# Another order for 2,801 steps: the copy of the sums of phi and v moves up in ScalarE's queue

## The chip, the cores and the metric

The kernel runs on one core of a Trainium2 chip. The metric is the device time of one execution in microseconds (us), lower is better, and the median of several runs is given. TensorE is named PE in the profile (PEld is its loading of weights), VectorE DVE, ScalarE ACT, GpSimd POOL and SyncE SP; SP issues nearly all the transfers between DRAM and the chip's memory.

## The reference

One layer in float32 over x of 2048 rows and 512 columns. Two halves, each with a layer norm, a scale and a shift from a small conditioning vector:

```python
mod = (silu(c) @ w_mod)                       # sa, ca, ga, sb, cb, gb: six rows of 512
h = layernorm(x) * (1 + ca) + sa
# A: linear attention, 32 heads of 16, with a learned feature map
pq, pk = q @ w_phi, k @ w_phi                 # per head
phi = concat([softmax(p), softmax(-p)])       # for q and for k: 32 features per head
kv, z = phi_k^T @ v, sum over rows of phi_k   # per head
A = (phi_q @ kv) / (phi_q . z + 1e-6)
x = x + ga * (A @ wo)
h = layernorm(x) * (1 + cb) + sb
# B: shift mixer and MLP
g = gelu(layernorm(h) @ w1)                   # four column groups shifted by +1, -1, +2, -2 rows
x1 = h + shifted(g) @ w2
B = x1 + gelu(layernorm(x1) @ w3) @ w4        # 512 -> 1376 -> 512
out = x + gb * B
```

## The kernel before

**Stages.** The rows are worked on in 8 chunks of 256 (two tiles of 128 rows). First stage, per chunk: norm, transposition, projection to k, v and q features (w_phi is folded into the weights ahead of it); per tile the products of the k features with v are summed on PE in one PSUM tile named `kva`, and the k features are summed in `za`. Only when all 16 tiles have been added can `kva` be read: ACT copies it to `kvs` (line "`act(kvs, kva)`" of the group "kvb"), PE spreads it out with four small products, and DVE multiplies the result with a mask into `const` (the matrix `kvb` of the code). Second stage, per chunk: the q features e, which went to DRAM, are loaded transposed by blocks, multiplied with the sums of the k features (`ez`) and reduced into the denominators (`pz`), normalised in place (`e`), turned by DVE (`pT`) and multiplied on PE with `kvb`; then wo, a norm, w1 with gelu, and the shift mixer with w2. Third stage, four times: the MLP for 512 rows, with seven products in place of eight for each pair of blocks (sums and differences of blocks first). Each float32 product in the large matmuls is made of three products of rounded high and low parts, so every operand has a "hi" (a copy) and a "lo" (source less hi).

**What sets the order.** The program is built in two passes. The first one records 2,801 steps (`plan.op`), each with its engine, its other possible engines and what it reads and writes; the step numbers are the same in both kernels. The second emits the steps in the order of a table `ORDER`, a list of step numbers written into the file. A letter behind a number (A, V, G) puts that step on ACT, DVE or POOL in place of its first engine. Each engine works through its own steps strictly in this order, so a step that waits holds up all that stand behind it on its engine. A second table, `SLOT`, says in which buffer every tile lies (one character for each tile of a name); a tile put into a used buffer waits until the last reader of the earlier tile is done.

```python
    def order(self):
        engines = {"A": "Activation", "V": "DVE", "G": "Pool"}
        for word in ORDER.split():
            o = self.ops[int(word.rstrip("AVG"))]
            if not word.isdigit():
                o.fn = o.alts[engines[word[-1]]][1]
            yield o
```

Names that the prediction uses: `qe` are the q features while they are made (`qt` is the copy of their projection; `q` and `k` with small shapes are minima, maxima and sums), `ke` the k features, `vv` the copy of v, `w` weights split in hi and lo, `ws` sums of blocks of w3 made for the third stage, `acc` the rows of the conditioning vector while they are summed up. Most of the helpers have one line each: L401 ACT's copies and exponentials, L418 DVE's and L420 POOL's two-operand operations, L442 DVE's reductions, L471 the matmuls.

Of the kernel before, what the change touches and what calls it, by code (L numbers as in the profile page):

```python
# [164 lines left out]
)  # L165
SLOT = {
    "pp": "015632614340517032150643012526242367251411661166312763426267553575313027152161025567307111272635"
          "0055072172642262056",
    "bd": "85",
    "w": "125634cd180254b6d83c72",  # L170
    "rk": "72634eg9",
# [1216 lines left out]
```

## Time and profile before

| | us |
|---|---|
| median of 3 runs | 558.26 (556.95 to 558.59) |
| the profiled execution's own time | 557.92 |
| its span, first to last instruction | 556.1 |
| PE busy | 545.4 (98% of the span) |
| DVE busy | 487.7 (88%) |
| ACT busy | 350.1 (63%) |
| POOL busy | 345.1 (62%) |

A row of the timeline gives the start in us from the span's beginning, the length of the group, engine, line, operation, output and inputs with their sizes, how many instructions were merged, and in square brackets the idle time of the engine before it with what ended that. A row of the windows gives, for a stretch, its length and the busy time of each engine in it. The granted clock of PE was 0.999 of full speed over the span.

### The profile page before, as it was taken

How to read it: one execution, taken by the hardware profiler on the slowest of the kernel's cores; microseconds unless marked ns; L12 is line 12 of the kernel's file. 1: busy time of each engine (PE TensorE's matmuls, PEld its weight loads, DVE VectorE, ACT ScalarE, POOL GpSimd, SP SyncE). 2: the span in 40 equal slices, each digit the busy share in tenths (PEclk: the TensorE clock that was granted, in tenths of full speed). 3: DMA queues.
4: the chain of work that ended last, by engine and by line, in shares of the span. 5: the costliest groups of instructions: out<-in, count | busy, mean ns of one | idle time of the engine just before them, and what ended most of it. 6: DMA issues, size and time to landing. Idle time of an engine off the chain costs nothing.

```text
span 556.1 us, 12353 instructions
## 1 busy us (share of the span) xinstructions
PE 545.4 (98%) x4498; PEld 488.6 (88%) x4498; DVE 487.7 (88%) x898; ACT 350.1 (63%) x831; POOL 345.1 (62%) x353
## 2 busy tenths in 40 slices
PE   8999999999989999999999999999999999999996
PEld 6988788888757788888889898999999999999996
DVE  3999999999999999999989867997878978786785
ACT  1899998635336778888888794966543365344530
POOL 2289976969489999999882655334332453333521
PEclk9999999999999999999999999999999999999999
DMA  8983366456447676779888798996678882972122
GB/s 317 366 279 133 127 197 226 154 153 181 156 126 255 207 204 196 248 242 312 267 262 272 245 306 297 383 326 211 276 238 308 286 330 66 294 246 81 57 78 76
DMA packets 63749, 124.90 MB, mean 225 GB/s; under 512 B 7140, under 2 KB 26852, under 8 KB 59592
## 3 DMA queue, kind: packets, MB, share of 16 engines
q1 hardware_dynamic: 63400, 124.04, 67.2%
q8 instruction: 35, 0.57, 0.4%
q14 instruction: 26, 0.21, 0.1%
q10 hardware_dynamic: 288, 0.07, 0.1%
HBM read 89.74 MB, written 34.35 MB: 223 GB/s over the span
## 4 chain that ended last, share of the span: by engine, by line
PE 86%; DVE 7%; DMA 3%; POOL 2%; issue 1%; DVEq 0%; ACT 0%; POOLq 0%
PE pp L471 36%; PE pa L471 27%; PE ac L471 20%; PE pt L480 2%; DVE pz L442 1%; DMA mod<-in_wmod 1%; DVE q L442 1%; PE kva L471 1%; POOL qe L420 1%; DVE pT L762 1%; DMA wr<-in_w 1%; POOL e L420 1%; DMA const<-in_id 1%; DVE ws L418 0%; DVE ez L418 0%
## 5 line engine op out<-in xcount | busy, mean ns | idle before, releaser
L471 PE MATMUL pp<-w,hh 128*128 128x512 f32 x576 | 138.3, 397 | 0.0
L471 PEld LDWEIGHTS pp<-w,hh 128*128 128x128 f32 x576 | 106.9, 188 | 25.6 <-issue 1.6
L471 PE MATMUL pa<-bH,wq 128*128 128x256 f32 x840 | 106.7, 282 | 0.0
L471 PE MATMUL ac<-w,gg 128*128 128x256 f32 x840 | 106.1, 281 | 0.0
L471 PEld LDWEIGHTS ac<-w,gg 128*128 128x128 f32 x840 | 103.2, 189 | 1.3
L471 PEld LDWEIGHTS pa<-bH,wq 128*128 128x128 f32 x840 | 103.1, 189 | 0.6
L471 PE MATMUL pa<-nT,w 128*128 128x256 f32 x384 | 48.6, 284 | 0.9 <-DVE nT L418 0.8
L471 PE MATMUL pp<-w,sh 128*128 128x512 f32 x192 | 49.4, 399 | 0.0
L471 PEld LDWEIGHTS pa<-nT,w 128*128 128x128 f32 x384 | 47.0, 191 | 2.6 <-DVE nT L418 1.4
L471 PE MATMUL pp<-w,oT 128*128 128x512 f32 x192 | 47.6, 396 | 0.4 <-DVE oT L418 0.4
L471 PEld LDWEIGHTS pp<-w,oT 128*128 128x128 f32 x192 | 35.5, 188 | 8.5 <-DVE oT L418 0.8
L471 PEld LDWEIGHTS pp<-w,sh 128*128 128x128 f32 x192 | 34.9, 188 | 8.0 <-issue 0.8
L420 POOL TENSOR_TENSOR gg<-cu,gg 128x128 fp32r<-128x128 f32 (+1 forms) x28 | 17.5, 633 | 36.4 <-PE ac L471 11.3
L401 ACT ACTIVATE gg<-sg 128x512 fp32r<-128x512 f32 x38 | 23.3, 624 | 22.6 <-DVE sg L418 12.4
L401 ACT ACTIVATE cu<-pa 128x512 f32<-128x512 f32 (+1 forms) x41 | 21.2, 522 | 25.9 <-PE pa L471 14.3
L588 POOL TENSOR_TENSOR rs<-mv,const 128x2 f32<-128x2 f32 x31 | 23.1, 748 | 19.0 <-ACT mv L595 18.3
L401 ACT ACTIVATE gg<-cu 128x128 fp32r<-128x128 f32 (+1 forms) x64 | 21.3, 354 | 18.7 <-PE ac L471 11.0
L420 POOL TENSOR_TENSOR w<-raw,w 128x512 fp32r<-128x512 f32 (+3 forms) x16 | 19.6, 1229 | 20.5 <-DVE w L410 12.0
L418 DVE TENSOR_TENSOR gg<-sg,gg 128x512 fp32r<-128x512 f32 x36 | 25.3, 706 | 7.8 <-PE pa L471 3.9
L420 POOL TENSOR_TENSOR ez<-e,const 128x1024 f32<-128x1024 f32 x12 | 29.0, 2419 | 4.1 <-ACT qe L401 4.1
L420 POOL TENSOR_TENSOR e<-e,q 128x1024 f32<-128x1024 f32 x16 | 30.9, 1946 | 0.6 <-DVE q L418 0.4
L420 POOL TENSOR_TENSOR ke<-ke,k 128x1024 f32<-128x1024 f32 x14 | 27.1, 1942 | 0.0
(215 smaller groups left out, 1208.0 us busy)
## 6 DMA issues: line engine op xcount, KB each, us to landing
wq<-dram SPq DMA_DIRECT2D x32, 1024.0 KB, 6.8
dram<-ws SPq DMA_DIRECT2D x35, 256.0 KB, 3.3
xl<-in_x SPq DMA_DIRECT2D x32, 256.0 KB, 3.4
dram<-qe SPq DMA_DIRECT2D x16, 512.0 KB, 2.9
e<-dram SPq DMA_DIRECT2D x64, 128.0 KB, 3.4
raw<-in_w SPq DMA_DIRECT2D x18, 256.0 KB, 3.2
mod<-in_wmod SPq DMA_DIRECT2D x16, 256.0 KB, 4.6
dram<-xl SPq DMA_DIRECT2D x16, 256.0 KB, 2.9
```

The lines of the kernel that those rows point to most:

```text
L401: nc.scalar.activation(o(), i(), func, **kw)
L418: dve = ("DVE", 71 + 1.04 * o.n + 90 * (isps(a) and isps(b)), lambda: nc.vector.tensor_tensor(o(), a(), b(), op=op))
L420: pool = ("Pool", cost, lambda: nc.gpsimd.tensor_tensor(o(), a(), b(), op=op))
L442: plan.op("DVE", 65 + 1.04 * a.n + 110 * isps(o), lambda: nc.vector.tensor_reduce(o(), a(), axis=AX.X, op=op), [o], [a])
L471: nc.tensor.matmul(o(), a(), b(), start=s, stop=e, **kw)
L480: nc.tensor.transpose(o(), i(), ident())
L588: plan.op("Pool", 540 + 10 * m, lambda: nc.gpsimd.tensor_tensor(r(), v(), mhalf[:, :m](), op=OP.pow), [r], [v, mhalf])
L762: plan.op("DVE", 71 + 1.04 * o.n, lambda: nc.vector.transpose(o(), i()), [o], [i])
```

## The change

`ORDER` and `SLOT` are replaced, and nothing else: the steps themselves, their shapes and the code that records them stay. 316 of the 2,801 steps get another engine (balanced: DVE has 871 steps where it had 866, ACT 734 where it had 737, POOL 347 where it had 349; PE's 521 and SP's 328 are the same steps in another order). Most steps move by a few places in their queues.

```diff
 ORDER = (
-    "1 10 3 42 0 4 35 2 50 54 5 52 56 23 36 31 9 11 88 85G 43 27 37 44 12 86 45 8 19 18 13 14 15 49G 38 39 51 100 "
...
-    "ez": "3622216688880646",
+    "ez": "4988322399990775",
...
```

ACT's queue at the end of the first stage, before. `kva` is the PSUM tile of the sums, `kvs` its copy; `qe` in place are exponentials, two for each tile of q; `qt` and `vv` are copies of projections, the first row is the copy of the sums of the k features.

```order
L401 ACTIVATE const_1854<-pp_1821 128x256
L401 ACTIVATE qe_1819<-qe_1819 128x32x16 x2
L401 ACTIVATE qt_1931<-pp_1892 128x512
L401 ACTIVATE vv_1956<-pp_1918 128x512
L401 ACTIVATE qe_1959<-qe_1959 128x32x16 x2
L401 ACTIVATE qt_2003<-pp_1938 128x512
L401 ACTIVATE kvs_2007<-kva_947 128x256
L401 ACTIVATE qt_2023<-pp_1990 128x512
```

The same place of ACT's queue after:

```order
L401 ACTIVATE const_1853<-pp_1817 128x256
L401 ACTIVATE qe_1826<-qe_1826 128x32x16
L401 ACTIVATE qt_1910<-pp_1889 128x512
L401 ACTIVATE w_1703<-raw_1805 128x512
L401 ACTIVATE qe_1826<-qe_1826 128x32x16
L401 ACTIVATE vv_1961<-pp_1912 128x512
L401 ACTIVATE qe_1959<-qe_1959 128x32x16
L401 ACTIVATE qt_1989<-pp_1942 128x512
L401 ACTIVATE kvs_2004<-kva_951 128x256
L401 ACTIVATE qe_1959<-qe_1959 128x32x16
```

Of the last pair of exponentials ahead of the copy `kvs`, one now stands behind it and one still ahead; the two of the pair before are parted by a copy of `qt` and one of a weight.

DVE's queue at the same place, before. `ez` are the two products with the sums of the k features, `pz` their reductions, `ws` and `w` are low parts for later stages, the last row is the minima and maxima that POOL's next step needs.

```order
L418 TENSOR_TENSOR qe_1819<-qt_1759,q_350_1789 128x1024
L418 TENSOR_TENSOR w_1735<-raw_1569,w_1605 128x512
L418 TENSOR_TENSOR ez_1873<-e_1678,const_1854 128x1024
L418 TENSOR_TENSOR ws_869<-ws_869 128x256
L418 TENSOR_TENSOR w_1607<-raw_1354,w_1475 128x512
L418 TENSOR_TENSOR ez_1912<-e_1486,const_1854 128x1024
L442 TENSOR_REDUCE pz_1916<-ez_1873 128x64
L442 TENSOR_REDUCE pz_1916<-ez_1912 128x64
L442 TENSOR_REDUCE q_370_1934<-qt_1931 128x32 x2
```

And after:

```order
L418 TENSOR_TENSOR w_1730<-raw_1436,w_1703 128x512
L418 TENSOR_TENSOR qe_1826<-qt_1755,q_345_1762 128x1024
L418 TENSOR_TENSOR w_1671<-raw_1295,w_1271 128x512
L418 TENSOR_TENSOR ez_1902<-e_1388,const_1853 128x1024
L418 TENSOR_TENSOR ez_1906<-e_1618,const_1853 128x1024
L442 TENSOR_REDUCE pz_1925<-ez_1902 128x64
L442 TENSOR_REDUCE pz_1925<-ez_1906 128x64
L442 TENSOR_REDUCE q_368_1930<-qt_1910 128x32 x2
```

The two low parts that stood between the two products are now done ahead of them.

A little further on in DVE's queue, up to the second `pT`, on which PE's first product of the second stage waits; before:

```order
L442 TENSOR_REDUCE q_383_2010<-qt_2003 128x32
L762 STREAM_TRANSPOSE pT_2013<-e_1678 128x1024
L442 TENSOR_REDUCE q_378_1968<-e_1951 128x64
L442 TENSOR_REDUCE q_383_2010<-qt_2003 128x32
L418 TENSOR_TENSOR const_2039<-pp_2018,const_229 128x256
L762 STREAM_TRANSPOSE pT_2041<-e_1486 128x1024
```

After:

```order
L442 TENSOR_REDUCE q_383_2011<-qt_1989 128x32
L762 STREAM_TRANSPOSE pT_2013<-e_1388 128x1024
L442 TENSOR_REDUCE q_383_2011<-qt_1989 128x32
L442 TENSOR_REDUCE q_389_2038<-qt_2023 128x32
L418 TENSOR_TENSOR const_2040<-pp_2017,const_781 128x256
L762 STREAM_TRANSPOSE pT_2044<-e_1618 128x1024
```

A reduction for another tile of q has come ahead of the second `pT`; the sum over `e` that stood between the two is done earlier, ahead of the first one.

More of the change, by code (lines that the diff above doesn't have):

```diff
@@ L40 @@
 ORDER = (
[124 rows of a table removed]
[124 rows of a table added]
 )
 SLOT = {
[L167 to L171, printed above, removed]
-    "xl": "10ikfbdb9h23j8l640adjlk9g876e46lfdil3j080678278h",
-    "st": "01b8h659g68cf15bdj7928gdc6g92if59",
-    "mv": "23fa07aej79eh68cf18f6bh7gbie5123a",
-    "rs": "54gd18ci13agj79eh2305a13e4jfb07ce",
-    "nm": "67ci9ej23b4dfh025b4di023a4gi05cd73ci06ahaeh14j894jd68bgh",
@@ L177 @@
-    "xn": "ac6e20j076ibfkic",
-    "mod": "dja8441l7ei4agf6ga",
-    "mod2": "0213",
-    "kva": "0",
-    "za": "6",
-    "hh": "0789abe7",
-    "pt": "72547173634774753001231627404702",
-    "raw": "9c3h5d79b2kfiche513a9hifgjl2",
-    "k1": "0114230103143431",
-    "ke": "4529730459817324",
-    "k2": "0451352502052531",
-    "vv": "h0ec840g7d05bh2b",
-    "qe": "7601181576971729",
-    "q1": "3252402454123154",
-    "qt": "2c30khikc02k",
-    "acc": "5kf1a",
-    "kvs": "2",
-    "pz": "4",
@@ L195 @@
-    "q2": "03125315",
-    "e": "0953845341605891",
-    "ez": "3622216688880646",
-    "q3": "1245043014204230",
-    "q5": "00032504",
-    "pT": "7466688584766450",
-    "oT": "96b3a9a6",
-    "nT": "a94baace",
-    "n": "6hh66h6hl5861454",
-    "h": "cia4ej0ckg72de3c",
-    "gf": "29470579",
-    "sh": "7e67edc7",
-    "pa": "371003132710576017436532106014275314360517374703257106341757",
-    "wr": "82032",
-    "ws": "d231ghe76gjgk921dff1b2haci9k6k1k55l",
-    "gb": "b",
-    "tw": "79265",
@@ L212 @@
-    "bL": "81374028",
-    "nb": "895d50a15424dg12",
-    "yt": "7fd13408i9df3723",
-    "bH": "64478207159823612653094704091721",
-    "tr": "k96hada5ikcl1hkl",
-    "wq": "739391ae09ae109e109ae091ea010e1a09e1",
-    "cu": "a10ki95f8j0jh81a6e4kk2l9d4g06ecj3f51k80l",
-    "gl": "lifhc6dj",
-    "ac": "45722570314275103624062315204736",
-    "gg": "95426980426801459802938176385986135927068341579637175369405638749056132790864257",
-    "sg": "hee3ae4ddlg325dd07ic8h71hik879h7d29l7h42",
-    "xb": "6cc7g43jf5gei0a9",
@@ L224 @@
-    "xc": "g4lg29lh522ihglc",
-    "uu": "li7al636",
+    "pp": "510234426360573046405216574732325716511600313075732270653365216523706542035040435752736700267672"
+          "4243153510404460571",
+    "bd": "46",
+    "w": "134625cd387165ad28cb09",
+    "rk": "73958dgc",
+    "xl": "01lif20gi5bh89hdfh4a36c0kejafg2h50eh36ecj9hl0aac",
+    "st": "03b8g32eh379c16aej5837hgb7h96dj2b",
+    "mv": "14fa06bdj2bdg379c16c68i2h9ie7064a",
+    "rs": "26hc17fi148hj2bdg34j2a19ef1c4f78e",
+    "nm": "57ei9dj54a89cg056afei0548fhi02bd54bd03aiaeg0fj581cg539hi",
@@ new lines @@
+    "xn": "ab75aj6ejag7f54b",
+    "mod": "ekbk73e1dj930hf2ke",
+    "mod2": "1023",
+    "kva": "4",
+    "za": "7",
+    "hh": "0789abe0",
+    "pt": "71713064136760724740255030200105",
+    "raw": "948hcla7b2l2g59fd34940abi351",
+    "k1": "0110502430210140",
+    "ke": "4501639451823940",
+    "k2": "5343025543253140",
+    "vv": "3246ekjhkfh0170l",
+    "qe": "7692282134682731",
+    "q1": "3242123515032015",
+    "qt": "ajj9ib759209",
+    "acc": "clf1e",
+    "kvs": "1",
+    "pz": "1",
@@ new lines @@
+    "q2": "03105351",
+    "e": "5617956458034928",
+    "ez": "4988322399990775",
+    "q3": "1245243214024032",
+    "q5": "44423145",
+    "pT": "3044399695373795",
+    "oT": "4a4ea04b",
+    "nT": "b05444be",
+    "n": "l12l4aaf1h5kje7g",
+    "h": "7519l62c7i1lfkcd",
+    "gf": "21535500",
+    "sh": "92be2cb0",
+    "pa": "720435033552357536277143075740636220453477601263027041460272",
+    "wr": "80061",
+    "ws": "010ie23c3782d1hgibgibgfbd0id69267k7",
+    "gb": "8",
+    "tw": "08935",
@@ new lines @@
+    "bL": "47604149",
+    "nb": "dgdj5dhj4gg4jbjd",
+    "yt": "9fje7gehj940707c",
+    "bH": "23820419431994595628147378657521",
+    "tr": "e10a2k3haldgbhd0",
+    "wq": "e90c934e174e3174e7314e7134e14317e431",
+    "cu": "672egi14hdfl25b7c1364hg9ked6l14g9cd0jblf",
+    "gl": "big235l6",
+    "ac": "26311637061227465013415304762351",
+    "gg": "25789138572584716831287609283795063284107962583265103241806937415809261809713458",
+    "sg": "kf6fka6k0j0k94h3la253c4b4acl7276ki2k97e4",
+    "xb": "9had9ei0fj3haf15",
@@ L226 @@
+    "xc": "5le904k6jhi2fg2i",
+    "uu": "00k2i6ck",
 }
```

247 rows, old and new, of the table ORDER are left out of this document.

## Prediction

> **What bounds the kernel now.** I read the page first: how busy each engine is and what the chain of work that ended last is made of; then the windows, to see in which stage that holds; then PE's waits one by one.
>
> ```profile
> span 556.1 us, 12353 instructions
> PE 545.4 (98%) x4498; PEld 488.6 (88%) x4498; DVE 487.7 (88%) x898; ACT 350.1 (63%) x831; POOL 345.1 (62%) x353
> ...
> PE 86%; DVE 7%; DMA 3%; POOL 2%; issue 1%; DVEq 0%; ACT 0%; POOLq 0%
> ```
>
> ```profile
> 0.00:11.80 11.80, 9.41 (x72) 7.99 (x72) 4.13 (x18) 1.49 (x2) 3.58 (x11) 1.00 0.86 302
> 11.80:144.00 132.20, 132.18 (x1014) 108.00 (x1018) 126.04 (x180) 100.62 (x231) 102.20 (x76) 1.00 0.62 203
> 144.00:206.00 62.00, 58.05 (x579) 46.00 (x572) 60.76 (x93) 35.32 (x78) 54.61 (x35) 1.00 0.62 194
> 206.00:551.80 345.80, 345.74 (x2839) 326.62 (x2838) 295.98 (x607) 212.70 (x521) 184.75 (x232) 1.00 0.71 237
> 551.80:556.10 4.30, 0.00 (x0) 0.00 (x0) 0.75 (x2) 0.00 (x0) 0.00 (x0) 0.81 0.37 124
> ```
>
> The columns behind each stretch are its length and the busy time of PE, PEld, DVE, ACT and POOL. PE is without a gap in two stretches, 132 and 346 us long. Its work is the same matmuls before and after, so 478 us can't get shorter by order; they can only get longer, by new waits. What order can win lies in the head (11.8 us), the middle stage from 144 to 206 us, and the tail (4.3 us). In the middle stage PE is busy for 58.05 of 62.00 us, but DVE for 60.76: there it is DVE that sets the pace. All that PE waited for, in us, times and longest:
>
> ```profile
> PE pp L471 <- ACT kvs L401: 1.5, 1, 1.5
> PE pp L471 <- DMA mod<-in_wmod: 1.4, 3, 1.0
> PE pp L471 <- DVE pT L762: 1.1, 1, 1.1
> PE pp L471 <- POOL const L498: 1.0, 1, 1.0
> PE pa L471 <- DVE nT L418: 0.8, 1, 0.8
> PE pp L471 <- DVE oT L418: 0.4, 1, 0.4
> ```
>
> The middle stage's four waits are kvs 1.48, pT 1.14, nT 0.78 and oT 0.40 us, 3.8 together (the first two exact from the rows that follow); that is the most that the stage can give.
>
> **The change part by part.** First the copy `kvs` that gives the change its name: PE and ACT around it.
>
> ```profile
> 144.00 1.52 PE L471 MATMUL kva<-ke,vv 128*32 128x64 f32 x96
> 153.99 0.65 PE L471 MATMUL kva<-ke,vv 128*32 128x64 f32 x32
> 154.57 3.04 PE L471 MATMUL pp<-w,hh 128*128 128x512 f32 x12
> 159.09 0.66 PE L471 MATMUL pp<-const,kvs 128*64 128x128 f32 x8 [1.48 <-ACT kvs L401]
> 163.86 1.16 PE L471 MATMUL pp<-pT,const 64*32 64x128 f32 x64 [1.14 <-DVE pT L762]
> ...
> 157.13 1.15 ACT L401 ACTIVATE qe<-qe 128x512 f32<-128x512 f32 x2 [5.15 <-POOL qe L420]
> 158.19 0.57 ACT L401 ACTIVATE qt<-pp 128x512 f32<-128x512 f32 x1
> 158.66 0.37 ACT L401 ACTIVATE kvs<-kva 128x256 f32<-128x256 f32 x1
> ```
>
> The sums are complete at 153.99 + 0.65 = 154.64, and the copy takes 0.37. It ran 4 us later because two exponentials stood ahead of it, and they waited for POOL's qe. PE was free at 154.57 + 3.04 = 157.61. The new queue takes one of the two exponentials out of the way (half of 1.15, so 0.57 us), but the other still waits for POOL, so the copy stays tied to POOL's start. That start hangs on DVE's minima and maxima, and these on the two `ez`:
>
> ```profile
> 143.83 0.68 DVE L418 TENSOR_TENSOR w<-raw,w 128x512 fp32r<-128x512 f32 x1
> 144.74 1.23 DVE L418 TENSOR_TENSOR ez<-e,const 128x1024 f32<-128x1024 f32 x1 [0.23 <-ACT const L401]
> 145.88 2.63 DVE L418 TENSOR_TENSOR ws<-ws 128x256 fp32r<-128x256 f32 x1
> 148.43 1.78 DVE L418 TENSOR_TENSOR w<-raw,w 128x512 fp32r<-128x512 f32 x1
> 150.13 1.21 DVE L418 TENSOR_TENSOR ez<-e,const 128x1024 f32<-128x1024 f32 x1
> 151.27 2.48 DVE L442 TENSOR_REDUCE pz<-ez 128x64 f32<-128x1024 f32 x2
> 153.66 1.27 DVE L442 TENSOR_REDUCE q<-qt 128x32 f32<-128x512 f32 x2
> 158.80 0.68 DVE L442 TENSOR_REDUCE q<-qt 128x32 f32<-128x512 f32 x1
> 162.57 1.23 DVE L762 STREAM_TRANSPOSE pT<-e 128x1024 f32<-128x1024 f32 x1
> ...
> 119.44 0.42 DVE L418 TENSOR_TENSOR ws<-ws 128x256 fp32r<-128x256 f32 x1
> ...
> 145.78 2.45 POOL L420 TENSOR_TENSOR ez<-e,const 128x1024 f32<-128x1024 f32 x1 [4.09 <-ACT qe L401]
> 148.19 1.47 POOL L420 TENSOR_TENSOR w<-raw,w 128x512 fp32r<-128x512 f32 x1
> 155.07 2.03 POOL L420 TENSOR_TENSOR qe<-qt,q 128x1024 f32<-128x1024 f32 x1 [5.41 <-DVE pz L437]
> ```
>
> A `ws` step takes 0.42 at 119.44 and 2.63 at 145.88, where it ends only after POOL's ez (145.78 + 2.45 = 148.23); the next `w` takes 1.78 in place of 0.68, and ends after POOL's w. So 2.21 + 1.10 = 3.3 us of DVE went into standing still beside POOL. The new order does these two steps earlier, leaving ez, ez. Their own 0.42 + 0.68 must be paid earlier on; what DVE had done up to the first ez is otherwise within a few tenths the same, since about as many steps of equal size left as came. Does the standing still vanish? POOL's ez and w are still there. Three cases:
>
> A. POOL's ez goes first, from about 144.7 (its input, the copy `const`, is ready 0.1 before DVE's own ez starts at 144.74). DVE's first ez runs from 147.2 to 148.3, POOL's w to 149.6, DVE's second ez to 150.7, against 150.13 + 1.21 = 151.34 before: 0.6 earlier.
> B. DVE's first ez goes first. The buffer table puts it behind the second of the three kva groups that start at 144.00, so from about 145.0 to 146.2; POOL's ez to 148.6, DVE's second ez to 149.8: 1.5 earlier.
> C. Nothing collides: 145.0 and two times 1.2 is 147.4, 3.9 earlier.
>
> By the Trainium skill, SBUF — State Buffer, Who interferes with whom, a DVE instruction with two SBUF inputs contends with a GpSimd instruction that reads SBUF. By that rule C needs POOL's ez to begin after 147.4, and A and B are what is left otherwise; the 2.63 against 0.42 agrees.
>
> Now to PE. The later minima ended at 153.66 + 1.27 = 154.93; from POOL's start at 155.07 to the end of kvs at 159.03 are 3.96 us, less the one exponential 3.39. A: minima 154.3, kvs done 157.8 to 157.9, and PE waits 0.3 in place of 1.48. B: minima 153.4, kvs done 156.9, no wait. But PE's next stop is pT, which DVE ended at 162.57 + 1.23 = 163.80, 8.87 after the minima. The new queue has one more reduction in that piece (0.60 between starts of such rows, 0.68 alone), so 9.47: A 163.8, B 162.9, against 163.80. PE, which comes to it earlier, waits there: its product with pT starts at 163.8 (A) or 162.9 (B), where it started at 163.86. **The wait is handed on:** 1.2 to 1.5 us taken from kvs come back as longer waiting for pT, and the net gain is 0.0 (A) to 0.95 (B). After that DVE's queue up to nT has no less work than before (the two low parts gone early, a copy of a projection come over from ACT), so nT and oT stay as they are, 0.4 and 0.8. POOL's new chance is two-sided: its buffer is now one that a store must leave first, which speaks for B, its early input for A. I take the middle, 0.4.
>
> The head: the last of the four large loads of w_mod is still behind the same transfers in SP's queue, and all six warming products of PE now run ahead of the first one. PE's real work starts with that load's last product, at 11.8. I cost this at nothing; bounds -0.3 and +0.3, since a 0.25 MB load at the 302 GB/s of the first window is 0.8 us and none is added. The identity for the transpositions is now loaded after the exponential on ACT; the head's slack covers it: PE transposes first at 12.4. The tail: the last six products' order gains 0.7 us for the last but one sums, but the last product, two DVE steps and the store behind it stay, so 4.3 remains.
>
> The two long stretches: zero waits before, and every one of the few hundred hand-overs has been dealt anew. I bound this from 0 to 2 us and put it at nothing in the likeliest case, since the same slack between engines (DVE 296 of 346, POOL 185) is there.
>
> Sum: 556.1 - 0.4 = 555.7 of span. The execution's own time is 557.92, 1.8 above its span, and the median 558.26 stands 0.34 above that: 558.26 - 0.4 = **557.9**.
>
> **The rivals.** *Faster: the waits really go* (C, or B with nT and oT also earlier). POOL's ez would have to be late: it needs the store of an earlier qe to land. DVE's minima are then bound by the copy of their projection, 151.0, pT comes at 160.5, PE is at its product at 161.3 and doesn't wait: 1.48 + 1.14 = 2.6 gained, 555.7. Against it: POOL stood idle 4.09 us before its ez, so it is there early, and it must lose by over 2 us.
>
> *Slower: a new wait on POOL's sums of the conditioning rows at 61 us.*
>
> ```profile
> 26.17 0.70 POOL L588 TENSOR_TENSOR rs<-mv,const 128x2 f32<-128x2 f32 x1 [0.67 <-DMA mod<-in_wmod]
> 28.89 0.69 POOL L410 TENSOR_SCALAR acc<-mod,const 128x512 f32<-128x512 f32 x1 [2.02 <-DVE xn L410]
> 30.21 1.29 POOL L420 TENSOR_TENSOR w<-raw,w 128x512 fp32r<-128x512 f32 x1
> 56.53 2.57 POOL L420 TENSOR_TENSOR acc<-acc,mod 128x512 f32<-128x512 f32 x2
> 61.06 1.07 PE L471 MATMUL pp<-acc,const 128*32 128x512 f32 x8
> ```
>
> The last sum ended at 59.10, PE came at 61.06: 1.96 of slack. The new queue puts in front of that sum one more sum (1.29), one more rs (0.70) and two roundings of w that another engine did (0.69 each): 3.4 us. If POOL's idle time (0.67 + 2.02 in these rows) takes it up, nothing happens; if none does, PE waits 1.4; if POOL's 2.02 wait also comes back in a new place, 3.5. From 1.96 us of lateness on, each us is one of time. Middle 2.4: 558.26 + 2.4 - 0.4 = 560.3. For it: POOL is nearly full between 40 and 60 us. Against it: both idle times lie ahead of it, and one is a wait for a load that now stands earlier in SP's queue.
>
> *The change doesn't do what it says*: one exponential still stands ahead of kvs, so if POOL's qe doesn't start earlier, the copy gains only 0.57, the product with pT nothing: 558.3. That is the end A of the likeliest case.
>
> **How the numbers follow.** Handed on (A, B, with small new waits): 0.58, 557.9, from 557.0 (B and a better head) to 559.5 (A and 1.2 of new waits). Faster: 0.24, 555.7. Slower: 0.18, 560.3. What a measurement of this kernel can tell from no change is 0.3%, 1.67 us: below 556.6 is faster, above 559.9 slower. Of the faster case 0.21 lies below 556.6, of the slower one 0.14 above 559.9, and of the likeliest 0.02 and 0.03 fall out on either side: faster 0.23, same 0.60, slower 0.17. The range leaves out about one in ten on each side: 555.5 to 560.2.
>
> **What would show it.** In the changed profile: PE's wait for kvs at most 0.4, its wait for pT 1.5 to 2.5, and its product with pT starting at 162.9 to 163.9; DVE's first ez or its second lengthened by 1 to 2.5 us beside POOL's ez; PE without waits from 12 to 144 and after 206, or with single ones under 1 us. The prediction is wrong if pT stops being waited for (then faster), or if a wait over 1.7 us stands in one of the two long stretches (then slower).

## The result, and the profile after

| us | before | after |
|---|---|---|
| median | 557.76 (6 runs, 556.95 to 558.59) | 554.89 (6 runs, 554.69 to 555.96) |
| span of the profiled execution | 556.1 | 552.9 |

The ratio is 0.995 (95% interval 0.9938 to 0.9963): 2.9 us faster. The forecast was 557.9, within 555.5 to 560.2, so the time came out below the range. The rival "the waits really go" (555.7, chance 0.24) lies nearest, but its sign did not come: PE still waits for pT, and longer. A second set of runs of the changed kernel, again beside the kernel before, gave 0.9936 (0.9914 to 0.9958).

The page of the profile after, with its first lines, the chain, and the list of what PE waited for:

```profile
span 552.9 us, 12370 instructions
...
PE 544.9 (99%) x4498; PEld 488.1 (88%) x4498; DVE 488.6 (88%) x903; ACT 351.7 (64%) x828; POOL 344.5 (62%) x351
...
PE 86%; DVE 7%; POOL 3%; DMA 2%; issue 1%; ACT 0%; DVEq 0%; POOLq 0%
```

```profile
PE pp L471 <- DVE pT L762: 1.7, 1, 1.7
PE pp L471 <- POOL const L498: 1.0, 1, 1.0
PE pp L471 <- DMA mod<-in_wmod: 0.7, 1, 0.7
PE pa L471 <- DVE nT L418: 0.7, 1, 0.7
```

The wait for kvs is gone and the wait for pT has grown from 1.14 to 1.72, as forecast. But the sum of PE's idle time fell from 6.2 to 4.1 by the two lists, where the forecast let it fall by 0.4; and 2.1 is still short of the 3.2 that the span lost. So part of the gain stands in no list of waits (0.54 of it lies behind PE's last product). It is found by laying the two traces side by side: PE does the same 4,498 matmuls in both, and at places where the same set of them is done, the difference of the start times is PE's lead. Rows of PE at such places, before and then after:

```profile
105.51 1.99 PE L471 MATMUL kva<-ke,vv 128*32 128x64 f32 x128
...
124.31 1.99 PE L471 MATMUL kva<-ke,vv 128*32 128x64 f32 x128
...
296.09 1.03 PE L480 MATMUL pt<-const,n 128*128 128x128 f32 x8
...
551.23 0.51 PE L471 MATMUL ac<-w,gg 128*128 128x256 f32 x3
```

```profile
104.58 1.55 PE L471 MATMUL kva<-ke,vv 128*32 128x64 f32 x96
...
109.05 0.65 PE L471 MATMUL kva<-ke,vv 128*32 128x64 f32 x32
...
123.85 1.99 PE L471 MATMUL kva<-ke,vv 128*32 128x64 f32 x128
...
162.47 1.16 PE L471 MATMUL pp<-pT,const 64*32 64x128 f32 x64 [1.72 <-DVE pT L762]
...
293.66 1.03 PE L480 MATMUL pt<-const,n 128*128 128x128 f32 x8
...
548.55 0.53 PE L471 MATMUL ac<-w,gg 128*128 128x256 f32 x3
```

The lead is 105.51 - 104.58 = 0.93 at the sums of the second group, 0.46 at 124, then 163.86 - 162.47 = 1.39 at the product with pT, 2.43 at 296 and 2.68 at the last product; the span ends 3.2 earlier. Done for all matmuls in both traces (equal work by the shortest time that each takes in either), with the value that the forecast gave to each stretch:

| stretch | forecast | measured |
|---|---|---|
| head (lead at 105 us) | 0 (-0.3 to 0.3) | 0.93 |
| 105 to 130 us | 0* | -0.48 |
| middle, up to the product with pT | 0.4 (A 0.0, B 0.95) | 0.97 |
| middle, oT and nT | 0 | 0.40 |
| 206 to 300 us | 0* | 0.62 |
| 300 us to the last product | 0* | 0.25 |
| behind the last product | 0 | 0.54 |

\* For all of the two long stretches together the forecast allowed 0 to 2 us of new waits, and no gain. The sum is 3.2. In the middle stage itself, DVE, POOL, ACT and PE after the change:

```profile
144.80 4.56 DVE L418 TENSOR_TENSOR ez<-e,const 128x1024 f32<-128x1024 f32 x2 [0.23 <-ACT qe L401]
149.29 2.48 DVE L442 TENSOR_REDUCE pz<-ez 128x64 f32<-128x1024 f32 x2
151.67 1.27 DVE L442 TENSOR_REDUCE q<-qt 128x32 f32<-128x512 f32 x2
...
145.46 2.82 POOL L420 TENSOR_TENSOR ez<-e,const 128x1024 f32<-128x1024 f32 x1 [5.13 <-DMA dram<-qe]
148.24 2.30 POOL L420 TENSOR_TENSOR w<-raw,w 128x512 fp32r<-128x512 f32 x1
...
153.09 2.03 POOL L420 TENSOR_TENSOR qe<-qt,q 128x1024 f32<-128x1024 f32 x1 [2.50 <-DVE pz L437]
...
156.18 0.37 ACT L401 ACTIVATE kvs<-kva 128x256 f32<-128x256 f32 x1
...
143.56 1.52 PE L471 MATMUL kva<-ke,vv 128*32 128x64 f32 x96
...
157.12 0.66 PE L471 MATMUL pp<-const,kvs 128*64 128x128 f32 x8
```

POOL's ez waited for a store of an earlier qe to land and began at 145.46, after DVE's first ez (144.80). That is case B. The two ez take 4.56 together, where two undisturbed ones take 2.4: the second stood still until POOL's ended at 148.28. It ended at 149.36 (144.80 + 4.56), 1.98 before the 151.34 of the old order; POOL's qe starts 1.98 earlier (153.09 against 155.07), and kvs is ready at 156.55, before PE comes to it at 157.12.

### The profile page after: what moved, and what is told of

It is laid out like the page before. It is cut to its first block, busy times and chain, and to the rows that moved or that the text cites. A ratio compares the mean times of both kernels' runs of the same rounds, so it can differ in the third digit from the quotient of the medians.

```text
span 552.9 us, 12370 instructions
## 1 busy us (share of the span) xinstructions
PE 544.9 (99%) x4498; PEld 488.1 (88%) x4498; DVE 488.6 (88%) x903; ACT 351.7 (64%) x828; POOL 344.5 (62%) x351
## 4 chain that ended last, share of the span: by engine, by line
PE 86%; DVE 7%; POOL 3%; DMA 2%; issue 1%; ACT 0%; DVEq 0%; POOLq 0%
PE pp L471 36%; PE pa L471 27%; PE ac L471 20%; PE pt L480 2%; DVE pz L442 2%; DVE q L442 2%; DMA mod<-in_wmod 1%; PE kva L471 1%; POOL qe L420 1%; DVE pT L762 1%; POOL ez L420 1%; POOL e L420 1%; DVE ez L418 1%; DMA const<-in_c 1%; DVE pp L437 0%
## 5 line engine op out<-in xcount | busy, mean ns | idle before, releaser
L471 PE MATMUL pp<-w,hh 128*128 128x512 f32 x576 | 138.8, 397 | 0.0
L471 PEld LDWEIGHTS pp<-w,hh 128*128 128x128 f32 x576 | 106.7, 188 | 26.1 <-issue 1.6
L471 PE MATMUL pa<-bH,wq 128*128 128x256 f32 x840 | 106.7, 281 | 0.0
L471 PE MATMUL ac<-w,gg 128*128 128x256 f32 x840 | 106.6, 281 | 0.0
L471 PEld LDWEIGHTS ac<-w,gg 128*128 128x128 f32 x840 | 103.4, 189 | 1.1
L471 PEld LDWEIGHTS pa<-bH,wq 128*128 128x128 f32 x840 | 103.1, 189 | 0.9
L471 PE MATMUL pp<-w,sh 128*128 128x512 f32 x192 | 49.4, 399 | 0.0
L471 PE MATMUL pa<-nT,w 128*128 128x256 f32 x384 | 48.3, 282 | 0.8 <-DVE nT L418 0.7
L471 PEld LDWEIGHTS pa<-nT,w 128*128 128x128 f32 x384 | 46.8, 188 | 2.5 <-DVE nT L418 1.2
L471 PE MATMUL pp<-w,oT 128*128 128x512 f32 x192 | 47.4, 395 | 0.0
L471 PEld LDWEIGHTS pp<-w,oT 128*128 128x128 f32 x192 | 35.4, 188 | 8.1 <-DVE oT L418 0.7
L401 ACT ACTIVATE gg<-cu 128x256 fp32r<-128x256 f32 (+1 forms) x56 | 19.1, 359 | 35.1 <-PE ac L471 19.7
L471 PEld LDWEIGHTS pp<-w,sh 128*128 128x128 f32 x192 | 34.6, 188 | 7.5 <-issue 0.8
L420 POOL TENSOR_TENSOR gg<-cu,gg 128x128 fp32r<-128x128 f32 (+1 forms) x26 | 15.8, 615 | 33.2 <-ACT gg L401 13.9
L420 POOL TENSOR_TENSOR e<-e,q 128x1024 f32<-128x1024 f32 x15 | 28.8, 1938 | 0.4 <-DVE q L418 0.2
L418 DVE TENSOR_TENSOR gg<-cu,gg 128x256 fp32r<-128x256 f32 (+1 forms) x54 | 22.1, 416 | 7.6 <-PE ac L471 4.6
```

What stands on the lines that cost most here:

```text
L401: nc.scalar.activation(o(), i(), func, **kw)
L418: dve = ("DVE", 71 + 1.04 * o.n + 90 * (isps(a) and isps(b)), lambda: nc.vector.tensor_tensor(o(), a(), b(), op=op))
L420: pool = ("Pool", cost, lambda: nc.gpsimd.tensor_tensor(o(), a(), b(), op=op))
L471: nc.tensor.matmul(o(), a(), b(), start=s, stop=e, **kw)
```

## The experiments

Each edit moves steps in the queues of one of the two kernels; numbers are step numbers, and nothing else is changed. Some of the edited files are one or two lines longer, and then the profile's line L471 reads L472 or L473.

**The copy alone.** ScalarE's queue of the kernel before; 463 and 462 are the exponentials, 466 the copy qt, 680 the copy kvs:

```diff
-463 462 466 680
+680 463 462 466
```

> The kernel before with one step moved: the copy kvs stands in ScalarE's queue ahead of both exponentials of the last q tile and of the copy qt. Theory (VectorE sets the pace of this stage): PE's wait for kvs (1.48 us) goes, its wait for pT grows from 1.14 to about 2.6, the product with pT starts at 163.8 to 163.9 as before, and the time stays within 0.2 us of before. Rival (the copy named in the change carries the gain): the product with pT starts 1.0 to 1.5 earlier and the time falls by 1.0 to 1.5 us.

Ratio 1.0015 (1.0005 to 1.0025). PE's list has no kvs any more, and this:

```profile
PE pp L472 <- DVE pT L763: 2.7, 1, 2.7
```

The whole 1.5 us came back at pT. PE's lead after that product is what it was ahead of the stage (0.43 from the head of this execution, 0.43 behind). The copy that gives the change its name is worth nothing by itself; the measured time is 0.15% longer.

**The two low parts alone.** DVE's and POOL's queues of the kernel before; 708 and 706 are the two ez, 784 ws and 672 w, 669 POOL's w, 461 its qe:

```diff
 DVE
-708 784 672 706
+708 706
 POOL
-669 461
+669 672 784 461
```

> The kernel before with the two low parts ws and w that stood between VectorE's two ez taken off its queue: GpSimd does them in its idle time of 5.4 us behind its own w. ScalarE's queue is that of before. Theory (the second ez sets when GpSimd's qe, the copy kvs and pT come): the second ez ends at about 149.3 in place of 151.35, stretched to 3.4 us beside GpSimd's ez; qe starts at 153.1 in place of 155.07; the product with pT starts at about 161.9 in place of 163.86; the time falls by 2.0 to 2.8 us. Rival (the wait is handed on to a later place): the product with pT comes earlier but nT and oT are waited for longer, and the time falls by at most 0.5.

Ratio 0.9975 (0.9956 to 0.9993), median 555.76. DVE and PE:

```profile
143.92 4.57 DVE L420 TENSOR_TENSOR ez<-e,const 128x1024 f32<-128x1024 f32 x2 [0.24 <-ACT const L403]
...
161.74 1.16 PE L473 MATMUL pp<-pT,const 64*32 64x128 f32 x64 [1.37 <-DVE pT L764]
```

This execution was 0.82 ahead from its head, so the product with pT came 163.86 - 161.74 - 0.82 = 1.30 earlier by the edit. The lead stands at 2.33 by 200 us (1.51 by the edit) and 2.09 by 213 us (1.27). A little less than the 2.0 expected, since DVE then waited 0.61 for a load of e; but the gain was not taken back by later waits, which the rival had forecast. With ScalarE's old queue, the two steps give what the whole change gives in this stage (1.37).

**The name undone.** The changed kernel, with the second exponential (463) ahead of kvs again:

```diff
 ScalarE
-462 466 680 463
+462 466 463 680
```

> The changed kernel with its name undone: the second exponential stands ahead of the copy kvs again. Theory (the place of the copy decides nothing once VectorE is earlier): the copy comes 0.6 later, PE waits 0.4 to 0.6 for it, its wait for pT falls from 1.72 to 1.1 to 1.3, the product with pT starts at 162.4 to 162.6 relative to the same head, the time stays within 0.2 of the changed kernel. Rival (the copy carries a part): 0.5 to 0.6 slower.

Median 555.00, ratio to before 0.9948 (0.9936 to 0.9960), where the changed kernel has 0.9950; PE's distance to the changed kernel is 0.29 ahead of the stage, from its head, and 0.29 behind it. My wait of 0.4 to 0.6 was a miss: the copy ended at 157.37 (156.99 + 0.38), 0.82 later than in the changed kernel, of which 0.29 are the head. The other 0.53 just fit into the 0.57 by which the copy had been ready ahead of PE (156.55 against 157.12), and PE started at 157.41 without a wait for it. The place of the copy decides nothing here either.

```profile
156.99 0.38 ACT L401 ACTIVATE kvs<-kva 128x256 f32<-128x256 f32 x1
...
157.41 0.67 PE L471 MATMUL pp<-const,kvs 128*64 128x128 f32 x8
...
162.76 1.16 PE L471 MATMUL pp<-pT,const 64*32 64x128 f32 x64 [1.71 <-DVE pT L762]
```

**Is pT what is left to gain?** The changed kernel; 716 is the second pT, 468 and 590 are reductions, 682 the product with the mask:

```diff
 DVE
-718 468 590 682 716
+718 682 716 468 590
```

> The changed kernel with the two reductions that stand ahead of the second pT in VectorE's queue put behind it; VectorE's work is the same. Theory (the stage is as long as VectorE's work in it, so that a wait moved by order alone comes back): the second pT ends 1.0 to 1.2 earlier, PE's wait for it falls from 1.72 to 0.5 to 0.7, its wait for nT grows from 0.66 to 1.6 to 1.9, the time stays within 0.2 of the changed kernel's. Rival (the wait for pT is what is left to gain): the time falls by 1.0 to 1.2.

Median 555.30, 0.47 slower than the changed kernel on the same chip (554.83).

```profile
PE pp L471 <- DVE oT L418: 1.5, 2, 1.3
...
PE pa L471 <- DVE nT L418: 0.7, 1, 0.7
PE pp L471 <- DVE pT L762: 0.5, 1, 0.5
```

The wait for pT fell as both theories said, but 1.5 us of new waits arose at oT, not at nT where I expected them: POOL's next qe needs one of the two reductions and waited 0.68 for it. Against the changed kernel PE won 1.19 at pT (0.12 behind ahead of the stage, 1.07 ahead at that product), lost 0.48 of it by 175 us and 1.28 more by 192 us. An order that moves DVE's work about, without making it shorter, hands the wait on, with a loss on top.

**Filling the time in which DVE stands still.** The changed kernel; 709 is the reduction pz of the first ez:

```diff
 DVE
-708 706 709 707
+708 709 706 707
```

> The changed kernel with one VectorE step moved: the reduction pz of the first ez goes between the two ez, so that VectorE does a step of one input while GpSimd's ez runs. Theory (VectorE's second ez stood still beside GpSimd's ez, 3.42 us in place of 1.21; a reduction does not): the reduction takes 1.2, the second ez starts at 147.2 and ends at about 149.5, the second pz ends at 150.7 in place of 151.77, the product with pT starts at about 161.4 in place of 162.47, and the time falls by 0.9 to 1.1 against the changed kernel. Rival 1 (the reduction is stretched beside GpSimd as well, or the second ez beside GpSimd's w): no gain, within 0.2. Rival 2 (handed on to nT): the product with pT comes earlier, the end does not.

Median 553.83 (553.46 to 554.20) against 554.83 (554.61 to 555.08) on the same chip; against the kernel before 0.9916 (0.9896 to 0.9936). It beats both kernels.

```profile
145.42 1.23 DVE L418 TENSOR_TENSOR ez<-e,const 128x1024 f32<-128x1024 f32 x1 [0.23 <-ACT qe L401]
146.68 1.23 DVE L442 TENSOR_REDUCE pz<-ez 128x64 f32<-128x1024 f32 x1
147.81 2.17 DVE L418 TENSOR_TENSOR ez<-e,const 128x1024 f32<-128x1024 f32 x1
...
146.10 2.80 POOL L420 TENSOR_TENSOR ez<-e,const 128x1024 f32<-128x1024 f32 x1 [5.14 <-DMA dram<-qe]
...
161.95 1.16 PE L471 MATMUL pp<-pT,const 64*32 64x128 f32 x64 [0.58 <-DVE pT L762]
```

While POOL's ez runs (146.10 to 148.90), the reduction with one input takes 1.23, as it does elsewhere, and the product with two inputs takes 2.17 instead of 1.23. PE was 0.61 behind the changed kernel ahead of this stage (its head) and 0.52 ahead of it behind: 1.13 gained, 1.07 still there at the end. By the Trainium skill, SBUF — State Buffer, Who interferes with whom, a reduction on this chip does not contend with GpSimd; the 1.23 agrees.

**What PE's change between kinds of products costs.** The kernel before; 147 to 212, 296 to 394 and 473 to 540 are groups of 32 small products for kva, the others projections of 12 large ones:

```diff
 PE
-147 148 210 212 364 435 373
+147 364 148 435 210 373 212
-296 298 392 394 565 574 518
+296 565 298 574 392 518 394
-473 475 538 540 385
+473 385 475 538 540
```

> The kernel before with PE's groups of 32 small products for the sums kva no longer in a row of four: seven of them are parted by one projection of 12 large products each, so that PE changes between the two kinds of product seven times more. No work is added. Theory (each such visit costs PE about 0.2 us that no wait shows): PE is 1.2 to 1.7 us later at 130 us with no new wait in the list, and the end is later by as much. Rival 1 (the visits cost nothing, and the slow loss between 100 and 130 us has another cause): no change there. Rival 2 (the delay is real but the stage that VectorE paces takes it up): 1.2 to 1.7 later at 130 us, the product with pT and the end within 0.3 of before.

Ratio 1.0058 (1.0041 to 1.0075). The list of waits is that of before, yet PE is 2.45 late by 140 us and stays so to the end. That is 0.35 for each of seven visits, more than I expected, and the stage that DVE paces takes none of it up. A group in the row of four takes (75.69 - 73.77) / 4 = 0.48, one by itself 0.58; the rest falls on the large products beside it: twelve of them take 2.99 here between two groups (77.36 - 74.37), and 2.81 on the mean of the 72 in a row between 107.44 and 124.31 before. What makes them longer no run isolates. Before, and then this experiment:

```profile
73.77 1.99 PE L471 MATMUL kva<-ke,vv 128*32 128x64 f32 x128
75.69 0.50 PE L471 MATMUL pp<-w,hh 128*128 128x512 f32 x1
```

```profile
73.79 0.65 PE L472 MATMUL kva<-ke,vv 128*32 128x64 f32 x32
74.37 3.06 PE L472 MATMUL pp<-w,hh 128*128 128x512 f32 x12
77.36 0.65 PE L472 MATMUL kva<-ke,vv 128*32 128x64 f32 x32
```

So the group that the changed kernel does alone at 109.05 explains most of its loss of 0.48 there: its lead falls from 0.93 ahead of the four groups to 0.58 just behind the lone one, by 0.35, and the other 0.11 go in small parts up to 124 us. Does the gain behind 206 us come the same way? The kernel before has one pair of products with pT (1134, 1135) parted by large ones (975):

```diff
 PE
-873 1134 975 1135 874
+873 975 1134 1135 874
```

> The kernel before with one PE step moved at 227 us: the two groups of products with pT that a projection parts stand together, as in the changed kernel. Theory (a visit costs 0.35 there too): PE is 0.3 to 0.4 earlier from 229 us to the end, with no wait gone from the list. Rival (the 0.35 belongs to the sums kva alone): no change at 229 us within 0.1. The time of an execution varies by more than this; the profile decides.

Before, and then this experiment, in which the two groups stand together behind the large products (in the changed kernel they stand ahead of them):

```profile
226.20 0.67 PE L471 MATMUL pp<-pT,const 64*32 64x128 f32 x32
226.80 0.96 PE L471 MATMUL pp<-w,sh 128*128 128x512 f32 x3
227.69 0.67 PE L471 MATMUL pp<-pT,const 64*32 64x128 f32 x32
228.28 0.96 PE L471 MATMUL pp<-w,sh 128*128 128x512 f32 x3
```

```profile
226.74 1.16 PE L471 MATMUL pp<-pT,const 64*32 64x128 f32 x64
227.82 0.97 PE L471 MATMUL pp<-w,sh 128*128 128x512 f32 x3
228.63 1.58 PE L471 MATMUL pa<-nT,w 128*128 128x256 f32 x12
```

PE's lead over before goes from 0.13 to 0.49 there and stays, with no wait gone: 0.36 of the 0.62 found between 206 and 300 us. The median was 556.90 (ratio 0.9988, 0.9980 to 0.9997).

The reverse for the sums did not pay. The changed kernel with its lone group put back:

```diff
 PE
-392 565 394
+392 394 565
```

> The changed kernel with one PE step moved: the products of the sums kva that stand alone between two projections (at 109 us) go back to their group of four, one visit fewer. Theory (a visit costs 0.35, by the seven visits that cost 2.45): PE is 0.35 earlier from 110 us to the end with the list of waits unchanged, and the time is 0.3 to 0.4 below the changed kernel's. Rival (the loss that the changed kernel shows between 100 and 130 us comes from elsewhere): no change within 0.1 in the profile.

The group's input was not there yet, and a wait came in place of the visit that was saved:

```profile
PE kva L471 <- ACT vv L401: 0.4, 1, 0.4
```

PE was 0.19 ahead of the changed kernel before it and 0.09 behind after it: 0.41 waited, 0.28 lost, so the saved visit gave back only 0.13 here, not 0.35. PE's granted clock was halved for 3.4 us in this execution, from 164.4 us, so its end says nothing; the runs spread from 553.19 to 556.28. A second set gave 554.50 to 555.48 in three executions, like the changed kernel and as the theory has it; a fourth, the profiled one, took 2,928 us, and nothing is read off it, so no profile decides between theory and rival, and the lowest runs of the first set stay unexplained.

> The kernel of the rejoined sums once more: its first profile fell on an execution in which PE's clock was halved for 3.4 us from 164.4 us, and showed the visit saved but a new wait of 0.4 for the copy vv in its place; its other executions were up to 1.5 us below the changed kernel. Theory (the new wait takes the saving back): a profile without that stretch shows PE within 0.2 of the changed kernel at 120 us and at the end. Rival (in those executions GpSimd's ez, which waits for a store, comes after VectorE's second ez, and nothing stands still): the second ez takes 1.2 instead of 3.4 and the end is 1.0 to 1.5 earlier.

With the reduction between the two ez as well:

> The changed kernel with the reduction pz between the two ez and with the sums rejoined. Theory (the parts add; the rejoining gives 0 to 0.35, the reduction 1.07): 1.0 to 1.4 below the changed kernel, 4.0 below the kernel before. Rival (the rejoining changes when GpSimd's ez starts and so what the reduction gains): 0.5 or less, or over 2.0, below the changed kernel.

Median 554.59, ratio 0.9953 (0.9936 to 0.9969): the same wait of 0.4 for vv (0.17 lost there, so 0.24 given back by the visit), 0.8 gained up to the product with pT, in all about 0.65 of lead over the changed kernel for the same head. The parts do not add to more; the reduction alone is the better kernel.

**The head.** The kernel before with the first transfers of the changed one and the steps that read them (SP's queue by its new order 35 52 2 42 50 54 56 237 23 31 19 88 27 100 92 236 96; on ScalarE's the identity, step 1, behind the exponential, 11):

```diff
 SP
-42 35 2 50 54 52 56 23
+35 52 2 42 50 54 56 237
 ScalarE
-1 0 11
+0 11 1
```

> The kernel before with the order of the first transfers of the changed kernel (17 on SyncE's queue, the identity behind the exponential on ScalarE's) and of the first few steps that read them (13 of VectorE, 10 of PE). Theory (the head's gain is real and is passed on): the last product with w_mod starts at about 10.8 in place of 11.82, PE is 0.9 to 1.0 ahead from there to the end, and the time falls by 0.9 to 1.0 us. Rival (the lead is swallowed where VectorE sets the pace): PE is 0.9 ahead up to 140 us, the product with pT starts at 163.7 to 163.9 as before, and the time stays within 0.3.

> The kernel with the changed head once more, since in its first profile PE fell back by 0.7 us evenly between 350 and 530 us with no wait, which no other execution shows. Theory (that was the execution, the head is worth 0.3 to 0.7 on the mean): no such falling back; the last product with w_mod at 10.7 to 11.4; the time 0.3 to 0.7 below before. Rival (the head is worth nothing on the mean): within 0.2 of before.

The same kernel twice: the last product with w_mod started at 11.11 and 10.63, and PE's lead of 0.71 and 1.19 passed through the middle stage unchanged (0.83 and 1.22 at 203 us). It is not swallowed there, since DVE's first ez itself waits for ACT's copy of sums that PE makes (143.97 in the first of these profiles, where it was 144.74). But the ratios are 0.9997 (0.9988 to 1.0005) and 0.9984 (0.9971 to 0.9997), less than that lead: in both profiles PE falls back by 0.7 to 0.8 between 230 and 530 us, in parts of some 0.01 us spread over many matmuls, with the same order and no wait. I had put this down to one execution; it came again, so it seems to belong to this kernel, and what in it does this stays open. The two parts of the head by themselves:

> The kernel before with one transfer moved: the identity is fetched behind the exponential on ScalarE's queue instead of first. Theory (the head's gain comes from the small loads no longer standing ahead of the large ones): the last product with w_mod starts 0.4 to 0.8 earlier than the 11.0 to 11.9 (mean 11.6) of the five executions with the old head, and the time falls by 0.3 to 0.6 us. Rival (it comes from SyncE's order): no change, 11.4 to 11.9.

> The kernel before with SyncE's first 17 transfers in the changed kernel's order and VectorE's four steps of statistics to fit; the identity stays first on ScalarE's queue. Theory (the identity decides): the last product with w_mod starts at 11.4 to 11.9 as before. Rival (SyncE's order decides): 10.7 to 11.2, and the time falls by 0.3 to 0.6 us.

Neither gives it, and each brought a wait for a step of POOL's that the whole does not have. With the identity alone moved the product started at 12.18 (ratio 0.9996, 0.9983 to 1.0008); PE's first product with w_mod stood 1.01 us for such a step there. With SP's order alone it started at 14.49 (ratio 1.0023, 1.0005 to 1.0040): PE stood 1.88 us from 7.6 us on for a small step of POOL's, and its granted clock was halved for 3.4 us from 10.2 us. How early the head is, is also a matter of the execution: six profiles with the old head show the product at 11.03 to 12.28 (mean 11.68), seven with that of the changed kernel at 10.69 to 11.44 (mean 10.99; 10.77 in the repetition of it, for which this was expected).

> The changed kernel once more, unaltered, beside the other three on the same chip: for a second profile of its head and tail. Theory (the head of the kernel before varied by 0.8 us from execution to execution with the same tables, so most of the 0.9 seen in the head is the luck of one execution): its last product with w_mod starts anywhere from 10.8 to 11.8. Rival (the changed head is earlier by itself): it starts at 10.8 within 0.2, here and in the three other kernels, which share that head.

So 0.7 of the 0.93 is the new head on the mean, with a spread from execution to execution of about 0.5 on either side.

**The tail.** The kernel before with PE's last ten products and DVE's last nine steps in the order of the changed one, and one sum (2784) on POOL:

```diff
 PE
-2773 2758 2774 2759 2746 2760 2771 2775 2772 2776
+2758 2759 2773 2774 2771 2775 2746 2760 2772 2776
```

> The kernel before with the end of the changed one: PE's last ten products in its order, one sum of GpSimd's in place of VectorE's, VectorE's last nine steps in its order. Theory (the order of the end brings the 0.5 us): from PE's last product to the end 4.1 us in place of 4.64, VectorE's last start 0.39 behind PE in place of 0.75. Rival (the 0.5 is a matter of the execution or of where the program's code lies, since kernels with the old end showed 4.11 and 4.47 too): 4.4 to 4.7 as in most executions of the old end.

From the start of PE's last product to the end it took 4.90, not 4.1. The other kernels with the old end show 4.64 to 4.66 (five) and 4.47, 4.11 and 4.20, and one 4.10; every one with the changed tables 4.09 or 4.10. DVE's last two steps, before and after:

```profile
552.22 0.75 DVE L418 TENSOR_TENSOR xb<-xb,ac 128x256 f32<-128x256 f32 x2 [0.67 <-PE ac L471]
```

```profile
549.19 0.75 DVE L418 TENSOR_TENSOR xb<-xb,ac 128x256 f32<-128x256 f32 x2 [0.84 <-PE ac L471]
```

They start about 0.75 behind the start of PE's last product before and 0.39 after, which makes 0.36 of the 0.54. All other profiles of the usual length have one of these two values, with the same waits; four profiles with the old order of the end have the 0.39 too. This experiment has the 0.39, as its theory said, but SP's long wait behind the issue of the last store took 1.91 in it, where it took 1.28 before and 1.31 after. So the order of the last steps does not by itself bring the 0.54; what does is not settled.

## Why the prediction was wrong

**Right.** DVE paces the middle stage, and the time goes with the two steps that stood between the ez and not with the copy (shown by the copy alone, the two low parts alone, and the name undone). The wait moved from kvs to pT. Case B came, with every time within 0.5 of its working: minima at 152.94 (153.4), kvs at 156.55 (156.9), the product with pT at 162.47 (162.9), and a lead won of 0.97 (0.95). The rest is the lead of 0.42 that PE brought into the stage; without it the three agree within 0.1. The Trainium skill's rule on the shared reads (SBUF — State Buffer, Who interferes with whom) held, since the second ez was stretched and the waits did not go by case C. That the rival of case C stood at 555.7, close to the 554.9 measured, is luck: what it named did not happen. The rival of POOL's sums at 61 us didn't come: the list has no such wait.

**Wrong, by its own steps.**
- "I take the middle, 0.4": between A and B there was no middle. POOL's ez comes either before or after DVE's first one. It came after it in the kernel before too (145.78 against 144.74, in the rows of the prediction), and case A had it come earlier than that. It waits for a store now, where it waited for an exponential, and I had named that and still halved the gain. Measured 0.97 of 0.95.
- "nT and oT stay as they are": the wait of 0.40 for oT went; no run isolates why.
- "I cost this at nothing; bounds -0.3 and +0.3" (head): 0.93 here and 0.7 on the mean. The last large load is the seventh transfer in SP's queue in both kernels; but its arrival, not its place, sets the start, and only SP's order, the place of the identity and the steps that read them together brought it. The bound of 0.3 did not follow from the 0.8 us that stood beside it, and the loads of w_mod are 512 KB each, twice the load that I reckoned with. With one profile, the spread of the head (1.2 us over six profiles with the old one) couldn't be seen, and the bound was too narrow.
- "478 us can't get shorter by order; they can only get longer, by new waits": refuted. A visit to another kind of product cost 0.35 in two trials with no wait in the list, and the change took one away behind 206 us and added one at 109. The Trainium skill, TensorEngine Tiling (Array Packing), Key Properties, says that a change of the tiling mode drains TensorE; the rows name 128\*32 and 64\*32 beside 128\*128, and the 0.35 would be what it comes to here, if that is the cause, which no run shows.
- "so 4.3 remains" (tail): 0.54 less, and not by the order of the last steps.

Terms that I had set to nothing came to 2.3 of the 3.2 (0.93 - 0.48 + 0.40 + 0.62 + 0.25 + 0.54); the one I sized came to 0.97 in place of 0.4. Of the 2.3, open are the tail, the 0.40 at oT, the 0.25 behind 300 us, and some 0.3 between 206 and 300. Between 206 and 300 us the changed kernel has no other visit fewer than the one tested. Behind 300 us its products fall into 44 stretches of one size where they fell into 47 (128\*128 by turns with 128\*96 and 96\*128); what such a change costs no run tests.

## What to carry to other kernels

Where one engine paces a stage, ask what shortens its work there: moving a wait by order only hands it on, but taking an operation with two inputs off its queue while GpSimd runs one, or putting a reduction in its place, gave 1.1 to 1.5 us. A matmul engine without idle time can still gain and lose by order, through the number of times that it changes the kind of product (0.35 us each in two trials here; undoing one saved 0.13 to 0.24 where it brought a wait). Lay two traces side by side by equal work before believing a list of waits, and take several profiles of one kernel before bounding a head that waits for transfers.

## Not expected of the hardware

- The cost of a visit: 0.35 us each on the mean of seven, 0.36 on another kind, shown in no wait.
- PE's granted clock was halved for 3.4 us twice within a run: from 10.2 us, 0.7 us after a stand of 1.88 had ended in the head, and from 164.4 us, 1.6 us after a wait of 1.96 had ended at the product with pT, where it cost 1.5 us. A wait of 2.68 at the same product, in the kernel with the copy alone, brought none.
- With PE's order unchanged behind the head, one kernel lost 0.7 us between 330 and 530 us in steps of some 0.01 us, in two executions alike.
